# Two mixtures of experts on one core: the first one's last quarter sums in SBUF, and its preparation work is emitted by a model that knows DMA

## The chip, the cores and the metric

The kernel runs on one core of a Trainium2 chip. The metric is the device time of one execution in microseconds (us). Below, TensorE does the matmuls, VectorE and ScalarE work on whole tiles, GpSimd helps with some subtractions and issues some DMAs, and SyncE issues most DMAs.

## The reference

Attention with two kinds of sparse mask (heads 0 to 3 local, heads 4 to 7 strided), then two dense mixtures of experts. All values are float32; the weights come as float64.

```python
x = attention(q, k, v)            # 4 batches x 576 tokens = 2304 tokens, 8 heads x 64 = 512 columns
h = x @ w_in                      # MoE 1: 512 -> 2048
g = h * np.tanh(softplus(h))      # mish
x = g @ w_out                     # 2048 -> 512
g = x @ w_gate                    # MoE 2: 512 -> 1536
val = x @ w_val
out = (silu(g) * val) @ w_out     # 1536 -> 512
```

## The kernel before

**Precision.** Every float32 operand is split into a high part (a rounded copy, made by ScalarE, `split_hi`) and a low part (the difference, made by VectorE or GpSimd, `split_lo`). One product is three matmuls (`mm3`, all recorded at L141): high x high, high x low, low x high.

**Weights.** The weights arrive as 64-bit tiles of 128 x 512. A *raw unit* (`w_ops`) makes one 32-bit tile of one raw tile: four VectorE operations (L348, L351, L356, L359), one squaring on ScalarE (L353), then the split (L131 on ScalarE, L136 on VectorE). A *sum unit* makes a sum or difference tile (`S12`, `S34`) of two weights that are there already: two half-width VectorE operations (L325 to L333), then the split. MoE 2 goes over its weights twice (token halves P = 0 and P = 1), so its units are stored to DRAM when they are first made (`wd`) and fetched again with `ld`.

**Tokens.** They stand in five chunks, four of 512 and one of 256. Chunks 0 and 1 are token half P = 0, chunks 2 and 3 are P = 1. The in-product of a half, a 2 x 2 block product, is done with seven products instead of eight (`PROD`), from sums of inputs (`T1` to `T4`, made by `t_items`) and of weights (`S12`, `S34`). Each of the seven is done for two groups of output columns, so a round holds 14 products in banks X, Y and Z. After the first three, ScalarE copies the bank as it stands (`k`, L986, in MoE 2 L1197); the next product adds to the same bank and must wait for that copy.

**MoE 1** (`middle`) goes over its 2048 inner columns in four quarters of 512. Quarters 1 to 3 hold: a round for one half (`in_round(q, A)`), the small chunk (`small_h`), three output phases (`y_phase`, one for each chunk of that half, then chunk 4), a round for the other half (`in_round(q, Z)`), and two output phases. Quarter 0's sums are stored to DRAM (`yd`); every later output phase copies its four banks with ScalarE (`yv`, L1039) and adds them to `yd` by an accumulating DMA of GpSimd's queue (L1045). The T tiles of a half are stored once and fetched back by ScalarE's queue (`t_load`, L1134) in the output phases ahead of the round that needs them. After the last round the sums are fetched from `yd` (L1114, L1121) and `operand` makes the seven operands of MoE 2's half P = 0 during the last output phase.

**Order of the work.** The instructions are emitted by hand in program order, and each engine and each DMA queue runs them in that order. What is not on TensorE's path stands in a list, `plan`, of raw units, sum units, T sums and gates (a gate holds the list until a stage of TensorE has been emitted). `fill` takes the head of the list as long as its end by a small model (`clk`: TensorE, VectorE and ScalarE, each with fixed costs) is before TensorE's; `need` runs the list on until a given weight is there. The model before has no DMA: a unit may be emitted before its raw tile has landed. `w_load` issues raw tiles from SyncE's queue as slots come free (`raw`, `ws`: two tiles each; a stored unit's target is a `ws` tile too). `W2_QUARTER` says how many units of MoE 2 each quarter takes.

**MoE 2** runs rounds r = 0 to 12; round r computes 256 inner columns of one half (`c_round`, and for P = 0 `c4_round` for chunk 4) and adds the outputs of round r - 1 (`d_tile`, L1261 on VectorE). The 36 units of MoE 2 that MoE 1 has not made are made here, one step behind every product (`w_late_step`; `LATE_ROUND` says how many units each round gets), and what is left is flushed ahead of the next round (`w_late_flush`).

Of the kernel before, what the change touches and what calls it, by code (L numbers as in the profile page):

```python
# [104 lines left out]
def local_strided_attention__mish_moe__swiglu_kernel(  # L105
# [15 lines left out]
    clk = {"pe": 0.0, "dve": 0.0, "act": 0.0}  # L121
# [26 lines left out]
    xh, xl, acc = {}, {}, {}  # L148
    for c, (t0, n) in enumerate(CHUNKS):
        xh[c] = sb.tile([128, 4, n], F32R, tag=f"xh{c}", name=f"xh{c}")  # L150
        xl[c] = sb.tile([128, 4, n], F32R, tag=f"xl{c}", name=f"xl{c}")

    def new_acc(c, a, n):
        acc[c] = sb.tile([128, a, n], F32, tag=f"acc{c}", name=f"acc{c}")
# [10 lines left out]
    w2list = w2_in("g", 0, "W0", "W1", "S12") + w2_out(0) + w2_in("g", 0, "S34") + w2_out(1, 2)  # L165
    w2list += w2_in("v", 0, "W0", "W1", "S12") + w2_out(3) + w2_in("v", 0, "S34") + w2_out(*range(4, 11))
    w2list += w2_in("g", 1, "W0", "W1", "S12") + w2_out(11) + w2_in("g", 1, "S34")
    for i in range(1, NP):
        for kind in "gv"[i == 1:]:
            w2list += w2_in(kind, i, "W0", "W1", "S12", "S34")  # L170
    wlist, plan, rtag = [], [], {}
# [11 lines left out]
    def put_w2(n):  # L183
        for _ in range(n):
            wlist.append(w2list.pop(0))
# [13 lines left out]
    put_w2(W2_QUARTER[0])  # L199
    for q in range(1, NQ):  # L200
# [7 lines left out]
        put_w2(W2_QUARTER[q])  # L208
# [15 lines left out]
    whole = set()  # L224

    def w_load(most=1):
        while most:
# [5 lines left out]
            if i < late["first"]:  # L233
# [8 lines left out]
                raws[i] = sb.tile([128, 512], I64, tag=tag, name="raw", bufs=2)  # L242
            else:
# [33 lines left out]
    def w_dest(i, key):  # L277
        if len(key) == 3:
            if i >= late["first"]:
                return w2_slot(key[0], key[1], key[2])  # L280
            return sb.tile([128, 2, 512], F32R, tag="ws", name="ws", bufs=2)
# [100 lines left out]
    def w_late_step():  # L382
        if not wq:
# [9 lines left out]
        while wq:  # L393
            op = wq.pop(0)
            op()
            if op is not w_hi:
                break

# [286 lines left out]
    def y_out(n, y, e):  # L685
# [9 lines left out]
        {"B11": "xh0", "T1": "xl0", "T2": "xh1", "B22": "xl1", "T3": "xh2", "B21": "xl2", "T4": "xh3"},  # L695
        {"B11": "xl3", "T1": "xh0", "T2": "xl0", "B22": "xh1", "T3": "xl1", "B21": "xh2", "T4": "xl2"},
    )
    tmp = [[], []]

    def operand(P, k):  # L700
# [3 lines left out]
        if k in ("T1", "T3"):  # L704
            tmp[k == "T3"] = [sb.tile([128, 512], F32, tag="pt", name="tt", bufs=4) for _ in range(2)]
        for j in range(2):
            if k[0] == "B":
                src = {"B11": y0[:, j], "B21": y0[:, 2 + j], "B22": y1[:, 2 + j]}[k]
            else:
                src = tmp[k == "T3"][j]  # L710
# [790 lines left out]
```

## Time and profile before

| | |
|---|---|
| median of 3 runs | 895.18 us (892.93 to 897.38) |
| the profiled execution | 891.74 us, of which the span is 890.0 us |
| mean granted clock of TensorE in it | 0.986 |
| busy: TensorE, its weight loads, VectorE, ScalarE, GpSimd | 96%, 80%, 69%, 51%, 21% |
| attention and quarter 0's first part | 0 to 117 us |
| MoE 1, quarters 0 to 3 | 117 to 472 us |
| MoE 2 | 472 to 890 us |

How to read it: the busy share of an engine is a mean over stages with different limits, so it only says who can be the bound. The idle time of TensorE, what ended it, and the granted clock of the same stretch are found in the waits and the windows. The rows are in microseconds from the span's start.

### The profile page before, as it was taken

The page shows a single profiled execution, that of the slowest core. Times are in us where ns is not written, and L with a number is a line of the kernel's source. Part 1 is how long each engine was busy: PE and PEld are TensorE (multiplying, and loading weights), DVE is VectorE, ACT ScalarE, POOL GpSimd, SP SyncE. Part 2 cuts the span into 40 slices and gives each one's busy share as a digit, 9 for nine tenths or more (in the row PEclk, how much of TensorE's full clock was granted, in tenths as well). Part 3 has the DMA queues.
Part 4 walks back from the last instruction along what each step waited for, and adds up shares of the span by engine and source line. Part 5 has one row for each costly group of instructions (what it writes and reads, how often), then busy time and mean ns, then how long its engine had stood idle before and what let it go on. Part 6 is the DMA issues. An engine that isn't in the chain of part 4 may idle for free.

```text
span 890.0 us, 14314 instructions
## 1 busy us (share of the span) xinstructions
PE 858.8 (96%) x5216; PEld 711.9 (80%) x5216; DVE 612.6 (69%) x1334; ACT 455.8 (51%) x1095; POOL 187.2 (21%) x210
## 2 busy tenths in 40 slices
PE   8999999989999989999698999999999999999998
PEld 5787778867888868788487888888888888888886
DVE  6998788667768648595458797978875635333534
ACT  7999955644756447465356544444443422332230
POOL 5643311002010010001014531212224312111211
PEclk9999999989999989999799999999999999999999
DMA  9865335634783694819679637566462563653322
GB/s 289 276 199 172 113 143 213 213 118 78 254 225 83 187 328 137 200 45 298 201 276 296 256 142 264 185 237 196 159 239 92 189 243 117 208 169 139 119 95 95
DMA packets 48166, 166.59 MB, mean 187 GB/s; under 512 B 5216, under 2 KB 8928, under 8 KB 45792
## 3 DMA queue, kind: packets, MB, share of 16 engines
q1 hardware_dynamic: 41328, 134.01, 43.6%
q0 software_dynamic: 5760, 25.17, 11.7%
q10 hardware_dynamic: 1008, 6.50, 2.1%
q8 instruction: 41, 0.67, 0.3%
q14 instruction: 29, 0.24, 0.1%
HBM read 104.32 MB, written 61.34 MB: 186 GB/s over the span
## 4 chain that ended last, share of the span: by engine, by line
PE 79%; DMA 8%; DVE 6%; ACT 4%; issue 1%; SPq 0%; POOL 0%; ACTq 0%; DVEq 0%; POOLq 0%
PE o L141 17%; PE y L141 14%; PE h L141 7%; PE cXg L141 7%; PE cXv L141 7%; PE cX L141 6%; DMA raw<-in_w_dram 5%; PE cZg L141 4%; PE c L141 3%; PE cZv L141 3%; PE cZ L141 3%; PE cYg L141 2%; PE cYv L141 2%; PE cY L141 2%; PE xp L575 1%; PE tp L538 1%
## 5 line engine op out<-in xcount | busy, mean ns | idle before, releaser
L141 PE MATMUL y<-g,w 128*128 128x512 f32 (+1 forms) x960 | 205.9, 372 | 5.6 <-ACT w L131 3.0
L141 PEld LDWEIGHTS y<-g,w 128*128 128x128 f32 x960 | 167.9, 190 | 37.7 <-DVE w L136 4.6
L141 PE MATMUL o<-wr,fs 128*128 128x512 f32 x648 | 149.6, 389 | 0.0
L141 PEld LDWEIGHTS o<-wr,fs 128*128 128x128 f32 x648 | 121.3, 188 | 25.0
L136 POOL TENSOR_TENSOR fs<-k,fs 128x512 fp32r<-128x512 f32 x36 | 49.4, 1372 | 260.2 <-ACT fs L131 181.8
L1261 DVE TENSOR_TENSOR acc<-acc,o 128x512 f32<-128x512 f32 x90 | 61.4, 685 | 36.5 <-PE o L141 36.2
L1045 POOL DMA_DIRECT2D yd<-yv x28 | 23.1, 824 | 293.9 <-ACT yv L1039 293.4
L131 ACT CAST fs<-k 128x512 fp32r<-128x512 f32 x36 | 22.4, 622 | 89.7 <-DVE k L1214 36.7
L141 PE MATMUL h<-xh,w 128*128 128x512 f32 (+1 forms) x208 | 61.5, 360 | 0.0
L141 PE MATMUL cXg<-T,wr 128*128 128x512 f32 x216 | 55.0, 390 | 2.8 <-ACT k L1197 2.8
L492 ACT ACTIVATE pt<-pt,sm 128x64 f32<-128x64 f32 (+1 forms) x160 | 55.9, 361 | 3.3 <-DVE sm L478 3.3
L141 PE MATMUL cXv<-T,wr 128*128 128x512 f32 x216 | 54.8, 389 | 0.0
L1200 DVE TENSOR_TENSOR k<-cZg,k 128x512 f32<-128x512 f32 x12 | 8.3, 692 | 67.0 <-PE cZg L141 67.0
L141 PE MATMUL cX<-xT,w 128*128 128x512 f32 x144 | 38.6, 418 | 12.9 <-ACT k L986 12.9
L141 PEld LDWEIGHTS cXg<-T,wr 128*128 128x128 f32 x216 | 40.4, 188 | 11.7 <-ACT k L1197 3.2
L1039 ACT COPY yv<-y 128x512 f32<-128x512 f32 x56 | 31.1, 589 | 33.4 <-PE y L141 23.1
L141 PEld LDWEIGHTS cXv<-T,wr 128*128 128x128 f32 x216 | 40.6, 188 | 8.4
L141 PEld LDWEIGHTS cX<-xT,w 128*128 128x128 f32 x144 | 28.6, 201 | 20.5 <-ACT k L986 14.5
L141 PEld LDWEIGHTS h<-xh,w 128*128 128x128 f32 x208 | 37.0, 189 | 5.2 <-issue 0.2
L521 POOL TENSOR_TENSOR pt<-pt,sm 128x192 f32<-128x192 f32 (+2 forms) x48 | 34.1, 730 | 16.6 <-DVE sm L514 13.0
L1197 ACT COPY k<-cXg 128x512 f32<-128x512 f32 x24 | 14.1, 589 | 43.8 <-PE cXg L141 43.8
L141 PE MATMUL h<-xl,w 128*128 128x512 f32 (+1 forms) x104 | 36.4, 350 | 0.0
(178 smaller groups left out, 1806.2 us busy)
## 6 DMA issues: line engine op xcount, KB each, us to landing
raw<-in_w_dram SPq DMA_DIRECT2D x50, 512.0 KB, 5.6
yd<-yv POOLq DMA_DIRECT2D x28, 512.0 KB, 8.5
wr<-wd_p SPq DMA_DIRECT2D x24, 512.0 KB, 5.0
rawl<-in_w_dram SPq DMA_DIRECT2D x18, 512.0 KB, 4.6
wr<-wd_g_S SPq DMA_DIRECT2D x16, 512.0 KB, 3.4
wr<-wd_v_S SPq DMA_DIRECT2D x14, 512.0 KB, 4.6
wd_p<-ws SPq DMA_DIRECT2D x12, 512.0 KB, 7.2
wr<-wd_g_W SPq DMA_DIRECT2D x10, 512.0 KB, 6.1
```

The lines of the kernel that those rows point to most:

```text
L131: nc.scalar.copy(hi, src)
L136: eng.tensor_tensor(out=lo, in0=src, in1=hi.bitcast(F32), op=ALU.subtract)
L141: nc.tensor.matmul(o, lhsT=lhs, rhs=rhs, start=first and i == 0, stop=last and i == 2, skip_group_check=more)
L492: nc.scalar.activation(out=pt[:, x], in_=pt[:, x], func=AF.Exp, scale=-1.0, bias=sm[:, 0, x:x + 1], accum_out=sm[:, 1, x:x + 1],)
L521: nc.gpsimd.tensor_tensor(out=a, in0=a, in1=sm[:, 1, x].unsqueeze(2).to_broadcast(a.shape), op=ALU.mult)
L538: nc.tensor.transpose(tp[:, 128 * x:128 * x + 128], a, ident)
L575: nc.tensor.matmul(banks[r][64 * h:64 * h + 64, o:o + nq - skip], lhsT=v_t[s][rows, i, 64 * h:64 * h + 64], rhs=ts[rows, c0 + skip:c0 + nq ...
L1039: on_act(COPY if nt == 512 else 0.4, clk["pe"], lambda: nc.scalar.copy(dst, p[:, :nt]))
L1045: nc.gpsimd.dma_start(yd[c][:, e0:e + 1], src, **kw)
L1197: nc.scalar.copy(t, p)
L1200: nc.vector.tensor_tensor(out=t, in0=p, in1=t, op=ALU.add)
L1261: nc.vector.tensor_tensor(out=acc[c][:, t], in0=acc[c][:, t], in1=o, op=ALU.add)
```

## The change

- **Units.** `W2_QUARTER` (5, 2, 8, 9 units of MoE 2 in MoE 1) gives way to the lists `early`: 2, 2, 6, 4, and 4 more behind the operands in quarter 3. So 18 units are made in MoE 1 instead of 24, and six (out-weights 1, 3, 5, 7, 8, 9) move into MoE 2: `LATE_ROUND` goes from (4, 8, 8, 8, 8) to (4, 9, 9, 9, 9, 2), and two steps follow each of the first three products when P = 0. The first two units are now out-weights 11 and 10, not in-weights and their sums.
- **The model.** `clk` gets SyncE, GpSimd's queue and the DMA engines. `moved` gives the time at which a transfer lands; a unit's first operation is not emitted by `fill` before its raw tile has landed by it, and a stored unit's split not before its target's earlier store has. TensorE's clock now also waits for weights, banks and operands (`pe_at`).
- **T sums.** `t_load` of the next half moves from the output phases into the round ahead (behind its third, fourth and sixth product), still on ScalarE's queue.
- **Quarter 3's sums.** The sums so far are fetched from `yd` ahead of each phase (`y_fetch`), and the phase adds its banks to them in SBUF with VectorE. The copies, the accumulating DMAs, and the fetches after the last round go, as do two 1 MB fetches in rounds 2 and 3 of MoE 2.
- **Operands.** The seven operands of P = 0 become items of `plan` (`op_items`): T1 and B11 behind the gate `y0`, the others behind quarter 3's last round. T2 is made as T3 + B11 instead of from T1. `small_operand` moves from round 0 of MoE 2 to quarter 3. The operands and final sums use other tiles (`SLOT`, `ACC`).
- **Start of MoE 2.** Units left over are filled in during round 0 (`w_rest`); round 1's weights are fetched behind round 0's sixth product.

```diff
-W2_QUARTER = (5, 2, 8, 9)
-LATE_ROUND = (4, 8, 8, 8, 8)
+LATE_ROUND = (4, 9, 9, 9, 9, 2)
+LATE_OUT = ((), (1,), (3,), (5,), (7,), (8, 9))
...
+ISSUE, LAND, MOVE, ADD_MOVE = 0.4, 2.1, 1.55, 2.7
...
+    def moved(queue, ready, halves=1, cost=MOVE):
+        if queue:
+            clk[queue] = max(clk[queue], ready) + ISSUE
+            ready = clk[queue]
+        clk["dma"] = max(clk["dma"], ready) + halves * cost
+        return clk["dma"] + LAND
...
+    early = [
+        w2_out(11, 10),
+        w2_out(0, 2),
+        w2_in("g", 0, "W0", "W1", "S12") + w2_out(4) + w2_in("g", 0, "S34") + w2_out(6),
+        w2_in("v", 0, "W0", "W1", "S12", "S34"),
+        w2_in("g", 1, "W0", "W1", "S12", "S34"),
+    ]
...
+            put_w2(q)
+            plan += [("gate", "y0"), ("op", "T1"), ("op", "B11")]
+            plan += [("gate", ("in", q, 1))] + [("op", k) for k in ("T3", "T2", "T4", "B22", "B21")]
+            put_w2(NQ)
...
     def hi_item(key, w, tf, ready):
+        def at():
+            r, k = slot_of.get(key, ([0, 0.0], 1))
+            return max(ready(), r[k])
+
         def do():
-            t = on_act(0.62, ready(), lambda: split_hi(nc.scalar, w[:, 0], tf))
+            t = on_act(0.62, at(), lambda: split_hi(nc.scalar, w[:, 0], tf))
             held.append((key, w, tf, t))
 
-        return (0.0, lambda: 0.0, do)
+        return (0.0, at, do)
...
-            items.append((cost, lambda: 0.0, do))
+            items.append((cost, lambda k=k: landed.get(i, 0.0) if k == 0 else 0.0, do))
...
+                if q == NQ - 1:
+                    x = acc[c][:, e]
+                    on = lambda: nc.vector.tensor_tensor(out=x, in0=x, in1=p[:, :nt], op=ALU.add)
+                    free(at, on_dve(0.69 if nt == 512 else 0.42, max(clk["pe"], landed["y", c]), on))
+                    continue
...
+    def y_fetch(c, tag, queue, bufs=1):
+        acc[c] = sb.tile([128, 4, CHUNKS[c][1]], F32, tag=tag, name="ys%d" % c, bufs=bufs)
+        (nc.scalar if queue == "act" else nc.sync).dma_start(acc[c], yd[c])
+        landed["y", c] = moved(queue, clk["pe"], 2 if c < NCH - 1 else 1)
...
-            in_round(q, A)
+
+            def behind_a(n):
+                if q > 1 and n in (2, 3, 5):
+                    t_load(Z, {2: "T1", 3: "T2", 5: "T3"}[n])
+
+            def behind_z(n):
+                if last and n == 2:
+                    y_fetch(3, "acc2", "act")
+
+            in_round(q, A, behind_a)
+            if last:
+                y_fetch(0, "xh0", "sp")
+                y_fetch(1, "xh1", "sp")
             small_h(q)
+            if last:
+                y_fetch(4, "v", "sp", 2)
...
+            if last:
+                gates["y0"] = clk["dve"]
             y_phase(q, 4, (0, 1, 2, 3))
-            in_round(q, Z)
+            if last:
+                small_operand()
+            in_round(q, Z, behind_z)
             if last:
                 w_late()
-                for c in (0, 1):
-                    new_acc(c, 4, 512)
-                    nc.sync.dma_start(acc[c], yd[c])
+                y_fetch(2, "acc3", "sp")
...
             if last:
-                drain()
-                new_acc(4, 4, 256)
-                nc.sync.dma_start(acc[4], yd[4])
...
-                at = (("B11", "T1"), ("T2", "B22"), ("T3", "B21"), ("T4",))
-                y_phase(q, 2, (0, 2, 1, 3), lambda i: [operand(0, k) for k in at[i]])
...
+                y_phase(q, 2, (0, 2, 1, 3))
...
                 w_late_step()
+                if n < 3 and P == 0:
+                    w_late_step()
...
-            if r in (2, 3):
-                new_acc(r, 4, 512)
-                nc.sync.dma_start(acc[r], yd[r])
...
                 def between(n):
-                    if r == 0 and n == 3:
-                        small_operand()
+                    if r == 0:
+                        if n == 5:
+                            if rest[0]:
+                                w_rest(True)
+                            ld(1, "W0", "S12", "S34")
+                        return
```

## Rows read from the trace of the kernel before

**Rows 1.** The page, part 1: busy time, share of the span, instructions.

```profile
PE 858.8 (96%) x5216; PEld 711.9 (80%) x5216; DVE 612.6 (69%) x1334; ACT 455.8 (51%) x1095; POOL 187.2 (21%) x210
```

**Rows 2.** Waits of PE, whole run: total us, times, longest us.

```profile
PE cX L141 <- ACT k L986: 12.9, 3, 8.8
PE y L141 <- ACT w L131: 3.0, 1, 3.0
PE cXg L141 <- ACT k L1197: 2.8, 1, 2.8
PE y L141 <- DVE w L136: 2.6, 2, 1.5
PE cZ L141 <- ACT w L131: 1.8, 1, 1.8
```

**Rows 3.** Windows: length; PE, PEld, DVE, ACT, POOL busy; clock, DMA share, GB/s.

```profile
186.72:222.98 36.26, 30.69 (x147) 25.09 (x145) 23.66 (x39) 15.30 (x28) 4.63 (x6) 0.91 0.46 104
223.00:242.05 19.05, 19.05 (x87) 15.76 (x86) 13.98 (x22) 14.28 (x25) 1.43 (x2) 1.00 0.82 291
...
316.88:342.75 25.87, 21.72 (x86) 16.96 (x85) 14.88 (x25) 12.69 (x25) 0.86 (x1) 0.87 0.81 247
...
385.90:419.50 33.60, 33.59 (x194) 29.45 (x192) 22.20 (x37) 15.59 (x29) 2.39 (x3) 1.00 0.64 200
419.50:450.43 30.93, 22.18 (x87) 17.74 (x86) 19.01 (x31) 16.68 (x31) 1.95 (x3) 0.83 0.59 174
450.43:472.19 21.76, 21.76 (x98) 18.02 (x97) 10.78 (x15) 9.75 (x17) 6.80 (x6) 1.00 1.01 340
```

**Rows 4.** The chain that ended last, 386 to 392 us: start, us, what.

```profile
386.06 5.75 PE h L141 x48
```

**Rows 5.** Timeline of ACT: start, us, instruction, idle time before and its releaser.

```profile
322.19 0.62 ACT L131 CAST ws<-wt 128x512 fp32r<-128x512 f32 x1 [5.70 <-DMA wd_v_S<-ws]
...
421.97 0.64 ACT L986 COPY k<-cX 128x512 f32<-128x512 f32 x1
433.52 0.68 ACT L353 ACTIVATE sq<-raw 128x512 f32<-128x512 f32 x1 [10.91 <-DMA raw<-in_w_dram]
```

**Rows 6.** Timeline of SyncE's queue around 184 us.

```profile
183.69 0.32 SPq L760 DMA_DIRECT2D wd_g_S<-ws  x1
184.18 3.64 SPq L248 DMA_DIRECT2D raw<-in_w_dram  x4
```

**Rows 7.** DMA issues, 395 to 436 us: count, KB each, median us to landing.

```profile
raw<-in_w_dram SPq DMA_DIRECT2D x5, 512.0 KB, 10.8
yd<-yv POOLq DMA_DIRECT2D x4, 512.0 KB, 9.6
wd_p<-ws SPq DMA_DIRECT2D x4, 512.0 KB, 9.1
```

**Rows 8.** DMA issues, whole run.

```profile
raw<-in_w_dram SPq DMA_DIRECT2D x50, 512.0 KB, 5.6
...
acc<-yd SPq DMA_DIRECT2D x4, 1024.0 KB, 8.9
...
acc<-yd SPq DMA_DIRECT2D x1, 512.0 KB, 14.8
```

**Rows 9.** VectorE groups (busy us, mean ns): two from 117:480, two from 539.2:693.

```profile
L351 DVE SCALAR_TENSOR_TENSOR wt<-raw,wt 128x512 int32<-128x512 int32 x40 | 27.7, 692 | 1.3
...
L348 DVE TENSOR_SCALAR wt<-raw 128x512 int32<-128x512 int32 x40 | 16.9, 422 | 24.0 <-DMA raw<-in_w_dram 24.0
...
L1261 DVE TENSOR_TENSOR acc<-acc,o 128x512 f32<-128x512 f32 x37 | 25.1, 683 | 3.2 <-PE o L141 2.9
...
L351 DVE SCALAR_TENSOR_TENSOR wt<-rawl,wt 128x512 int32<-128x512 int32 x12 | 11.5, 955 | 0.2
```

**Rows 10.** Windows: one round of MoE 2 (round 3).

```profile
577.60:616.00 38.40, 38.40 (x193) 32.78 (x192) 32.80 (x55) 16.65 (x30) 8.18 (x6) 1.00 0.63 219
```

**Rows 11.** Timeline of VectorE in the same round.

```profile
587.38 0.69 DVE L1200 TENSOR_TENSOR k<-cZg,k 128x512 f32<-128x512 f32 x1 [4.60 <-PE cZg L141]
```

More of the change, by code (lines that the diff above doesn't have):

```diff
@@ L181, in put_sums, with put_w2 @@
             plan.append(("unit",))
-    def put_w2(n):
-        for _ in range(n):
-            wlist.append(w2list.pop(0))
+    def put_w2(x):
+        for key in early[x]:
+            wlist.append(key)
             plan.append(("unit",))
@@ L704, in operand @@
         if k in ("T1", "T3"):
-            tmp[k == "T3"] = [sb.tile([128, 512], F32, tag="pt", name="tt", bufs=4) for _ in range(2)]
+            tmp[k] = [sb.tile([128, 512], F32, tag="pt", name="tt", bufs=4) for _ in range(2)]
         for j in range(2):
@@ L859, in t_items, with op_items, vec_item, pair_items @@
         return with_split(items), lo("T4", z1)
-    t_rest = []
+    def op_items(k):
+        y0, y1 = acc[0], acc[1]
+        t = sb.tile([128, 2, 2, 512], F32R, tag=SLOT[0][k], name=k)
+        ops[0][k] = t
+        if k in ("T1", "T2", "T3"):
+            tmp[k] = [sb.tile([128, 512], F32, tag="pt", name="tt", bufs=4) for _ in range(2)]
+        items = []
+        for j in range(2):
+            if k[0] == "B":
+                src = {"B11": y0[:, j], "B21": y0[:, 2 + j], "B22": y1[:, 2 + j]}[k]
+            else:
+                src = tmp["T2" if k == "T4" else k][j]
+                x3 = tmp["T3"][j] if k != "T1" else None
+                in0, in1, op = {
+                    "T1": (y1[:, j], y0[:, j], ALU.subtract),
+                    "T3": (y1[:, 2 + j], y1[:, j], ALU.subtract),
+                    "T2": (x3, y0[:, j], ALU.add),
+                    "T4": (y0[:, 2 + j], src, ALU.subtract),
+                }[k]
+                items.append(vec_item(src, in0, in1, op))
+            items += pair_items(t[:, j, 0], t[:, j, 1], src, (nc.gpsimd, nc.vector)[j])
+        return items
+    def vec_item(out, in0, in1, op):
+        do = lambda: nc.vector.tensor_tensor(out=out, in0=in0, in1=in1, op=op)
+        return (SPLIT, lambda: 0.0, lambda: on_dve(SPLIT, 0.0, do))
+    def pair_items(hi, lo, src, eng):
+        at = [0.0]
+        def do_hi():
+            at[0] = on_act(0.62, clk["dve"], lambda: split_hi(nc.scalar, hi, src))
+        def do_lo():
+            if eng is nc.vector:
+                on_dve(SPLIT, at[0], lambda: split_lo(eng, lo, src, hi))
+            else:
+                clk["pool"] = max(clk["pool"], at[0]) + 2 * SPLIT
+                split_lo(eng, lo, src, hi)
+        return [(0.0, lambda: 0.0, do_hi), (SPLIT, lambda: at[0], do_lo) if eng is nc.vector else (0.0, lambda: 0.0, do_lo)]
+    def w_rest(last=False):
+        clk["dve"] = max(clk["dve"], clk["pe"] - 0.6)
+        fill()
+        if last:
+            drain()
+        if last or not head() and not behind:
+            assert not head() and not behind and not held
+            rest[0] = None
+            w2_tiles("ws", 2, ("W1", 1, "g"), ("W1", 1, "v"))
+            w2_tiles("raw", 2, ("p", 0), ("p", 1))
+            ld(0, 0, 1)
     def head():
@@ L869, in head @@
             kind, *x = plan[0]
+            if kind == "op" and behind:
+                bg.extend([hi_item(*behind.pop(0)), lo_item()])
+                return bg[0]
             if kind == "gate":
@@ L1061, in middle @@
             clk[k] = 0.0
-        whole.update([("i", QF), ("i", QF + 2)] + [("o", f) for f in range(QF)])
+        for r in turns.values():
+            r[1:] = [0.0, 0.0]
+        landed.update((i, 0.0) for i in list(landed))
+        whole.update((k, 0.0) for k in [("i", QF), ("i", QF + 2)] + [("o", f) for f in range(QF)])
         def h_plain(n, f):
@@ L1153, in ld @@
                 t = w2_slot(kind, r, x)
-                if kind != "p" and P == 0 and i > (kind == "g"):
+                if P == 0 and (2 * i + x in sum(LATE_OUT, ()) if kind == "p" else i > (kind == "g")):
                     continue
```

159 lines of the change are left out of this document (100 added, 59 removed).

## The prediction

> **What bounds the kernel now.** I read the page first. TensorE is busy for 96% of the span [rows 1], so only its idle time, and time at a lower clock, can be won. The waits of TensorE, grouped, say who ended that idle time [rows 2]: ScalarE copies of product banks, 12.9 us in three waits, then splits of weights, 3.0 and 2.6, then a copy at the start of the second mixture of experts (MoE 2), 2.8, then 1.8. Next the stretches of MoE 1. Equal work stands in several of them, so the undisturbed one measures the others [rows 3]. A round of seven products on one token half takes 19.05 us undisturbed; quarter 2's second round takes 25.87 (6.8 lost) and quarter 3's second round 30.93 (11.9 lost). The small chunk's products and three output phases take 33.60 in quarter 3, of which the products are 5.75 [rows 4], so the phases take 27.85; in quarter 1 they take 36.26 (8.4 lost). With the wait of 1.8 ahead of quarter 3 and the 2.8 in round 0 of MoE 2 [rows 2], 8.4 + 6.8 + 1.8 + 11.9 + 2.8 = **31.7 us** are lost. That is more than the waits: in the stretches that hold them the granted clock is 0.91, 0.87 and 0.83 on average and 1.00 in the others [rows 3], so some matmuls ran at the lower of the two levels.
>
> Then what ended those waits. ScalarE stood for 10.91 us before the squaring of a raw weight tile that had not landed [rows 5]; the copy of the next bank was queued behind it, and TensorE waited for that copy. In quarter 2 it stood 5.70 us before a split whose target was still being written to DRAM [rows 5]. In quarter 1 the late raw out-weights were issued at 184.18, right behind a store that SyncE's queue issued at 183.69 [rows 6]. Engines run in order, so an operation emitted before its data is there holds everything behind it. Around quarter 3's wait a raw tile took 10.8 us to land, a store 9.1 and an accumulating store 9.6 [rows 7]; over the whole run a raw tile takes 5.6 [rows 8].
>
> **The change, part by part.** *Fewer units in MoE 1.* A raw unit is 0.42 + 4 x 0.69 = 3.2 us of VectorE [rows 9], a sum unit, two half-width operations and one whole, 2 x 0.42 + 0.69 = 1.5. Ahead of quarter 1 two raw units stand in place of three raw and two sums: 6.4 instead of 12.6 us. The late out-weights may be issued only when every earlier stored unit is split, so their issue at 184.18 moves ahead by these 6.2 or more, and 8.4 shrinks to between 0 and 4 (what a second late tile could cost, 9.6 less the 5.6 of a median one); I take 1.5, nearer to 0, since 6.2 is most of 8.4. In quarter 2 six units stand for eight, in quarter 3 four (and four behind the operands) for nine: in each a megabyte or more read, and as much stored, leaves the stretch in which raw tiles took 10.8.
>
> *Emission by a model with DMA.* A unit enters the engines' order only when the model says that its raw tile has landed (0.4 + 1.55 + 2.1 = 4.05 us, plus its queue) or that its target's store is done. Where that comes true no copy is held; where DMA is later than the model, it is held for the difference. It has slack: a round of 19.05 us is 14 products of 1.36, and a bank's copy is made after the first of them and needed before the fifth, so 3 x 1.36 less the copy's 0.64 [rows 5] = 3.4 us. At the median of 5.6 the error is 1.6 and hidden; at 10.8 it is 6.7, and 3.3 of it show. Quarter 2's 6.8 becomes 0 to 6.8; I take 2.5, nearer to the median. The wait of 1.8 comes behind output buffers whose accumulating stores are not finished; quarter 2 keeps these stores, so it stays.
>
> *Sums in SBUF in quarter 3.* Nine accumulating stores and 20 ScalarE copies go; 16 VectorE additions of 0.683 [rows 9] and 4 half-width ones of about 0.42 come, 12.6 us over 33.60 + 19.05 + 21.76, in which VectorE is busy for 22.20, 13.98 (the undisturbed round) and 10.78 [rows 3]. That is room enough, and units leave besides. Their cover is that the five old sums are there in time. Such a fetch took 8.9, and 14.8 at worst [rows 8]; the first two are issued at the end of a round, 5.75 + 27.85/2.5 = 16.9 us before the first phase's end, where its additions stand. If the cover is gone, a late sum holds VectorE and with it four banks. SyncE waits for the round's end before these fetches, and raw tiles queue behind them, whose users are a phase later. Quarter 3's 11.9 becomes 0 to 6 (half, if the second of two late tiles stays); I take 2.
>
> *T sums fetched during products.* The three 1 MB fetches move on ScalarE's own queue from the output phases into the round ahead, each issued when its tile's last reader is a product old, so that nothing behind it is held; they leave the phases where raw tiles and accumulating stores compete. The Trainium skill, "DMA: Bandwidth & Descriptors", section "Issuing engines are not separate DMA queues", says that transfers started by any engine run on the same 16 DMA engines and interleave. By that rule their queue hides nothing, only the earlier time does, and quarter 2 could keep its whole 6.8, the upper end above; the trace's 10.8 beside other queues' transfers agrees with it.
>
> *Operands of MoE 2.* The first two are made inside quarter 3's last round, the others during its last two phases, from sums that are whole since quarter 3's first half; before, all seven stood in the last phase and ended in the 2.8 wait. Count and kind of the operations stay. 2.8 becomes 0 to 2.8; I take 1, because units that are left now overlap round 0, and round 1's fetched weights are issued only after its sixth product, 2.72 + 5.75 = 8.5 us ahead of use, where a raw tile of that size takes 5.6.
>
> *Six units later.* Rounds 1 to 4 of MoE 2 get one more raw unit each. A round is 38.40 us with VectorE busy for 32.80 in 55 instructions [rows 10]. Five more are 3.0 us at that mean, and 4.8 if each took the 0.955 that L351 takes there [rows 9]: 35.8 to 37.6, under 38.40. An idle 4.60 us of VectorE [rows 11] lies in the first three products, where the change puts two steps for one. So 0, or at worst 1 per round; I take 1 in all, and 1 more for left steps flushed ahead of round 1. The Trainium skill, "SBUF — State Buffer", section "Who interferes with whom", says that a VectorE operation with two SBUF inputs contends with a GpSimd one that reads SBUF. By that rule L351's 0.955, against 0.692 in MoE 1, is such waiting, and a unit put where GpSimd is idle costs 3.2; the sum would stay.
>
> **Sum.** Left are 1.5 + 2.5 + 1.8 + 2 + 1 + 1 + 1 = 10.8 us, so 20.9 go. The profiled execution took 891.74 (890.0 of it span), which gives 870.8. The median of the runs is 895.18, 3.4 above it; as a third of the waits stays, I keep a third of that: **872.0**. Bounds: with all 31.7 gone 860.0; with the upper ends left (4 + 6.8 + 1.8 + 6 + 2.8 + 4 + 1 = 26.4) 886.4, and with the same share of 3.4, 889. What is late next is then TensorE itself.
>
> **The rivals.** *The model is too early.* Its 4.05 against 10.8 leaves 3.3 us per raw tile on TensorE, and as a wait of 8.8 [rows 2] lost 11.9 in all, 4.4 with the clock. Three such tiles in quarters 2 and 3 add 13: 885. For it: the accumulating stores of quarters 1 and 2 stay. Against: fewer bytes there. *It doesn't do what it says.* The order of emission comes out much as before, since a matmul that needs a unit forces it anyway, and a wait for the forced weight takes the place of each wait for a copy: about 893. Against: the raw tile that cost 10.91 was for a unit that only MoE 2 reads. *Slower.* The plan is a strict list, and a head that the model holds back holds the weights behind it. In quarter 2 six units share two target tiles: three turns of a store and a raw tile, at 9.1 + 10.8, are 60 us of the 33.60 + 19.05 + 21.76 = 74 in which four raw and four sum units for quarter 3 must follow (18.8 us). From 74 on they come as a burst ahead of a round, with TensorE waiting for all of it; in two quarters that is 37.6 on 872, about 909. Against: eight units fitted into the same stretch before.
>
> **How the numbers follow.** Chances: the forecast (861 to 881) 0.65, the model too early (881 to 889) 0.19, no effect 0.08, slower 0.08. About 0.5%, 4.5 us, is what a measurement of this kernel can tell from no change; so faster 0.84, same 0.08, slower 0.08. The range 861 to 889 leaves out the last two and a little below.
>
> **What would show it.** In the new profile: quarter 3's second round at 19 to 21 us, and no ScalarE wait of over 5 us for a raw tile; the out-weights of quarter 1 issued well before 184; additions of 0.69 on VectorE in quarter 3 and no accumulating store; rounds 1 to 4 at 38.4 with VectorE busy for 36 to 37. Wrong would be waits of VectorE for the fetched sums, rounds above 39, or the same waits for other tiles.

## The result, and the profile after

The changed kernel takes **865.46 us** (median of 4 runs, 863.77 to 871.11). The kernel before, measured beside it, takes 894.28 (892.93 to 897.38). The ratio is 0.9684 (95% interval 0.963 to 0.9738), a gain of 28.8 us. The profiled execution of after is the longest of its four: 871.11 us, of which the span is 869.3, at a mean granted clock of 0.994; the other three took 863.77 to 866.90, at 0.998 to 1.000. Against the 891.74 of before's profiled execution it gained 20.6. All rows of after below are of this longest execution.

The page of after, part 1 (busy time, share of the span, instructions), answers to [rows 1]:

```profile
PE 855.0 (98%) x5216; PEld 710.7 (82%) x5216; DVE 619.6 (71%) x1354; ACT 448.5 (52%) x1075; POOL 177.2 (20%) x201
```

ScalarE has 20 instructions fewer and VectorE 20 more: the copies and additions of quarter 3. Next the waits of TensorE in after, from 117 to 700 us (total us, times, longest us), beside [rows 2]:

```profile
PE cXg L160 <- DVE k L1344: 4.7, 2, 3.3
PE cXg L160 <- DMA wr<-wd_g_W: 1.0, 1, 1.0
...
PE cZ L160 <- ACT w L150: 0.6, 1, 0.6
```

The waits of 12.9, 3.0, 2.8 and 2.6 are gone. Of the kind that was 1.8 ahead of quarter 3 (`cZ`, a weight's split), 0.6 stands in quarter 2. Waits stand there that before did not have, in MoE 2 (`cXg`), for VectorE and for a fetched weight. The windows of after (length; busy PE, PEld, DVE, ACT, POOL; clock, DMA share, GB/s) answer to [rows 3] and [rows 10]: quarter 1's phases, quarter 2's second round, quarter 3's phases and second round, then rounds 1 and 2 of MoE 2.

```profile
190.40:217.95 27.55, 27.55 (x146) 23.79 (x145) 21.86 (x37) 13.99 (x26) 5.14 (x7) 1.00 0.50 105
312.40:331.40 19.00, 19.00 (x85) 15.73 (x85) 9.23 (x14) 13.15 (x23) 0.86 (x1) 1.00 0.58 177
378.40:406.00 27.60, 27.60 (x147) 23.76 (x146) 22.15 (x39) 9.87 (x18) 1.30 (x1) 1.00 0.46 169
406.10:425.20 19.10, 19.10 (x86) 15.80 (x85) 9.93 (x17) 13.44 (x24) 4.97 (x5) 1.00 0.16 56
471.80:517.10 45.30, 40.92 (x193) 34.03 (x194) 40.36 (x69) 19.45 (x37) 9.23 (x7) 0.96 0.66 239
517.10:555.50 38.40, 38.40 (x194) 32.77 (x193) 36.00 (x61) 17.79 (x33) 7.76 (x6) 1.00 0.58 206
```

The 36.26 of quarter 1 is 27.55, the 25.87 of quarter 2 is 19.00, the 30.93 of quarter 3 is 19.10, and the clock is back at 1.00 in all three. Round 1 of MoE 2 stands out: 45.30 for the 38.40 that the next round takes.

The table sets every kernel of this study against the undisturbed length of each stage (in its heading, us), from the starts of TensorE's groups. What stands in it is time lost; blank is under 0.3. "q2 2nd" is quarter 2's second round, and so on; "r0" is round 0's in-products with its chunk 4, "r1" round 1's in-products, "r2, r3" those of rounds 2 and 3 together. Two losses lie outside its columns: 0.8 in quarter 2's first round in after, and the in-products of round 5, 1.7 in after and 1.7 to 2.1 in the other kernels with the units moved, but 4.5 in the last row. The stages are those of the one profiled execution of each kernel, the median is of all its executions.

| kernel | q1 phases 27.54 | q2 2nd 19.07 | q3 1st 19.47 | q3 2nd 19.07 | last phases 21.76 | r0 24.79 | r1 19.04 | r2, r3 38.08 | median us |
|---|---|---|---|---|---|---|---|---|---|
| before | 8.7 | 6.8 | 1.9 | 11.9 | | 3.8 | | | 894.28 |
| **after** | | | | | | 1.1 | 5.8 | | 865.46 |
| e1 no model | | | | | | 0.6 | 3.6 | | 866.71 |
| e2 model alone | 7.5 | | 8.4 | | 4.4 | 13.8 | | | 893.86 |
| e3 T fetches late | | | | | | 1.0 | 4.9 | | 866.33 |
| e4 units back | 7.1 | | 4.5 | | | 6.9 | 1.6 | | 880.49 |
| e5 sums in DRAM | | | | | | 4.9 | | 3.6 | 868.40 |
| e6 out-weight 1 early | | | | | | 2.1 | | | 863.86 |
| e7 units alone | | 2.2 | | 9.1 | | 5.9 | | 3.2 | 881.15 |
| e8 five units first | 7.6 | | | | | 0.9 | 5.7 | | 874.53 |
| e9 units, model | | 0.4 | | | 4.9 | 13.7 | | 2.8 | 882.81 |
| e10 units, sums | | 2.3 | 0.3 | | | 1.1 | 5.8 | | 868.89 |
| e11 fetch order | | | | | | | 1.8 | | 863.12 |
| e12 units, T fetches | | | | 4.1 | | 4.9 | | 3.9 | 875.35 |

### The profile page after: what moved, and what is told of

Same layout as the page of the kernel before. It is cut to its first block, busy times and chain, and to the rows that moved or that the text cites. A ratio compares the mean times of both kernels' runs of the same rounds, so it can differ in the third digit from the quotient of the medians.

```text
span 869.3 us, 14259 instructions
## 1 busy us (share of the span) xinstructions
PE 855.0 (98%) x5216; PEld 710.7 (82%) x5216; DVE 619.6 (71%) x1354; ACT 448.5 (52%) x1075; POOL 177.2 (20%) x201
## 4 chain that ended last, share of the span: by engine, by line
PE 87%; issue 5%; DMA 3%; DVE 2%; ACT 1%; POOL 1%; SPq 0%; POOLq 0%; ACTq 0%; DVEq 0%
PE y L160 18%; PE o L160 17%; PE h L160 8%; PE cXg L160 7%; PE cXv L160 7%; PE cX L160 6%; PE c L160 4%; PE cZv L160 4%; PE cZg L160 3%; PE cZ L160 3%; PE cYv L160 2%; PE cYg L160 2%; PE xp L617 2%; PE tp L580 2%; PE cY L160 2%
## 5 line engine op out<-in xcount | busy, mean ns | idle before, releaser
L160 PE MATMUL y<-g,w 128*128 128x512 f32 (+1 forms) x960 | 202.3, 369 | 0.0
L1173 POOL DMA_DIRECT2D yd<-yv x20 | 16.1, 803 | 189.2 <-ACT yv L1167 189.2
L1167 ACT COPY yv<-y 128x512 f32<-128x512 f32 x40 | 23.0, 589 | 29.1 <-PE y L160 23.3
L563 POOL TENSOR_TENSOR pt<-pt,sm 128x192 f32<-128x192 f32 (+2 forms) x48 | 33.8, 724 | 17.9 <-DVE sm L556 11.9
L155 DVE TENSOR_TENSOR wr<-wt,wr 128x512 fp32r<-128x512 f32 x42 | 33.7, 801 | 5.1 <-ACT wr L150 5.0
L150 ACT CAST wr<-wt 128x512 fp32r<-128x512 f32 x42 | 25.8, 614 | 22.1 <-DVE wt L370 12.9
```

Source lines behind the costliest of these rows:

```text
L150: nc.scalar.copy(hi, src)
L155: eng.tensor_tensor(out=lo, in0=src, in1=hi.bitcast(F32), op=ALU.subtract)
L160: nc.tensor.matmul(o, lhsT=lhs, rhs=rhs, start=first and i == 0, stop=last and i == 2, skip_group_check=more)
L563: nc.gpsimd.tensor_tensor(out=a, in0=a, in1=sm[:, 1, x].unsqueeze(2).to_broadcast(a.shape), op=ALU.mult)
L1167: t = on_act(COPY if nt == 512 else 0.4, clk["pe"], lambda: nc.scalar.copy(dst, p[:, :nt]))
L1173: nc.gpsimd.dma_start(yd[c][:, e0:e + 1], src, **kw)
```

## The experiments

Two theories were put to the test first. **M:** the emission by a model that knows DMA wins the time, by keeping a unit out of the engines' order until its data is there. **U:** the amount of work wins it, since six fewer units in MoE 1, and two instead of five ahead of quarter 1, leave room whatever the order. Sums in SBUF and T fetches are smaller parts by both.

**The model taken out** of the changed kernel: nothing lands late by the model, and no unit waits for it.

```diff
     def moved(queue, ready, halves=1, cost=MOVE):
-        if queue:
-            clk[queue] = max(clk[queue], ready) + ISSUE
...
+        return 0.0
...
-        return (0.0, at, do)
+        return (0.0, lambda: 0.0, do)
```

> The changed kernel with the model's DMA taken out: transfers cost nothing in it, a unit is emitted whether its raw tile has landed or not, TensorE's clock waits for nothing. Units, sums in SBUF and early fetches stay. Theory M (the order of emission is what won MoE 1's time): the ScalarE waits for raw tiles come back, quarter 2's and 3's second rounds are 4 to 12 us over 19.05 again and the median is 875 to 890. Theory U (fewer units and fewer bytes won it): rounds stay at 19 to 21, the median within 4 us of 865.5.

866.71 us (865.0 to 867.55), ratio 0.97 (0.9679 to 0.972): within about a microsecond of the changed kernel. With all other parts there, the model is not needed.

**The model alone**, put into the kernel before (24 units in the order before, DRAM sums, T fetches in the phases, one step behind each product).

```diff
-            items.append((cost, lambda: 0.0, do))
+            items.append((cost, lambda k=k: landed.get(i, 0.0) if k == 0 else 0.0, do))
```

> The kernel before with the model alone: 24 units in MoE 1, accumulating stores in all quarters, fetches of T sums in the output phases, operands in the last phase, one step behind every product in MoE 2. Theory M: 15 to 25 us of the 28.8 are won with it, the median is 870 to 880, and what stays lost is the 1.8 ahead of quarter 3 and the 2.8 at the start of MoE 2. Theory U: 0 to 8 us are won, 886 to 894.

893.86 us (891.39 to 896.58), ratio 1.0006 (0.9993 to 1.002). Waits of TensorE, 121 to 600 us:

```profile
PE cXg L160 <- ACT k L1335: 7.9, 1, 7.9
PE cXg L160 <- ACT B L150: 4.3, 1, 4.3
PE y L160 <- ACT w L150: 2.9, 1, 2.9
PE cX L160 <- ACT w L150: 2.8, 1, 2.8
```

The second rounds of quarters 2 and 3 run undisturbed, as intended, and ScalarE's waits for raw tiles in MoE 1 fall from 27.7 us in before to 1.3. But 7.5 us stay in quarter 1, 8.4 appear ahead of quarter 3, 4.4 in the last phases and 13.8 at the start of MoE 2: TensorE waits there for splits of weights (the last two lines), an operand and a copy. The held units come later, and the same time is lost there. Theory M falls.

**24 units in MoE 1 again**, with all other parts of the change.

```diff
-LATE_ROUND = (4, 9, 9, 9, 9, 2)
-LATE_OUT = ((), (1,), (3,), (5,), (7,), (8, 9))
+LATE_ROUND = (4, 8, 8, 8, 8)
+LATE_OUT = ((),) * 6
...
-        w2_out(11, 10),
-        w2_out(0, 2),
+        w2_in("g", 0, "W0", "W1", "S12") + w2_out(0) + w2_in("g", 0, "S34"),
+        w2_out(1, 2),
```

> The changed kernel with the units as before: 5, 2, 8, 9 of MoE 2 in the four quarters (five of the last behind the operands), 4 and four times 8 in MoE 2's rounds 0 to 4. Theory M: MoE 1 loses 0 to 5 us, and round 1 of MoE 2, which took 45.3 in the changed kernel, is back near 38.4 to 40, so the median is 860 to 868. Theory U: MoE 1 loses 10 us or more in quarters 1 to 3, the median is 872 to 885.

880.49 us (879.52 to 881.19), ratio 0.9855 (0.984 to 0.987): 15 us are lost again, in quarter 1 (7.1), ahead of quarter 3 (4.5) and in round 0 (6.9). So the units decide more than any other part that was taken out. The edit changes two things, how many units there are and which come first; the kernel with five units first, below, takes the second alone.

**Quarter 3's sums in DRAM again**: accumulating stores, the fetches after the last round and in rounds 2 and 3, the operands in the last phase, and the start of MoE 2 as before. In this run and in the later one that adds the sums in SBUF, these go together; no run takes them apart.

```diff
-                if q == NQ - 1:
-                    x = acc[c][:, e]
-                    on = lambda: nc.vector.tensor_tensor(out=x, in0=x, in1=p[:, :nt], op=ALU.add)
-                    free(at, on_dve(0.69 if nt == 512 else 0.42, max(clk["pe"], landed["y", c]), on))
-                    continue
...
+                y_phase(q, 2, (0, 2, 1, 3), lambda i: [operand(0, k) for k in at[i]])
```

> The changed kernel with quarter 3's sums added in DRAM again, fetched behind its last round, and the operands made in its last output phase; model, units and early T fetches stay. Theory M: quarter 3's second round stays at 19 to 22 us, only the 2.8 at the start of MoE 2 and a little more come back: 866 to 872. Theory S (the accumulating stores of quarter 3 are what made its raw tiles late): that round is 5 to 12 us longer, 873 to 882.

868.4 us (867.19 to 870.93), ratio 0.9724 (0.9704 to 0.9745). Quarter 3 stays undisturbed, so theory S of the text above does not hold with the other parts there; round 0 loses 4.9, and rounds 2 and 3, which fetch two of the sums, 3.6, while round 1 gains its 5.8 back, though it has the ninth unit too.

**Five units ahead of quarter 1**, 18 in all as in the changed kernel.

```diff
-        w2_out(11, 10),
-        w2_out(0, 2),
+        w2_in("g", 0, "W0", "W1", "S12") + w2_out(0) + w2_in("g", 0, "S34"),
+        w2_out(2, 4),
```

> The changed kernel with one thing altered: which of its 18 units of MoE 1 come ahead of quarter 1. Five (three raw, two sums, the selection of the kernel before) instead of two; as many fewer later (5, 2, 3, 4 and 4). All else stays: model, T fetches, sums in SBUF. Theory U (the work put ahead of a stage decides): quarter 1's phases, 27.53 us in the changed kernel, are again 34.6 to 36.3, as in the kernel before (36.26) and with the units put back (34.64), so 7 to 8 us are lost: 872 to 874. Theory M (the emission model keeps work away from a stage that has no room): phases below 30, time 864 to 868.

874.53 us (873.2 to 875.85), ratio 0.9781 (0.9763 to 0.98). Its quarter 1 in a window, and SyncE's queue in it and then in after:

```profile
187.60:222.70 35.10, 30.17 (x146) 25.00 (x146) 25.98 (x43) 15.81 (x29) 5.16 (x7) 0.90 0.48 107
```

```profile
184.52 0.32 SPq L807 DMA_DIRECT2D wd_g_S<-ws  x1
185.00 3.65 SPq L284 DMA_DIRECT2D raw<-in_w_dram  x4
```

```profile
171.12 0.33 SPq L807 DMA_DIRECT2D wd_p<-ws  x1
171.61 3.94 SPq L284 DMA_DIRECT2D raw<-in_w_dram  x4
```

Five units put the four raw out-weights behind a store at 184.52, as in [rows 6]; with two they go at 171.61. That one list is worth 9 us of the 15 that the units put back had cost, and the model, which is on in this kernel, does not help it.

**The units alone**, put into the kernel before with the second step behind the first products.

```diff
-W2_QUARTER = (5, 2, 8, 9)
-LATE_ROUND = (4, 8, 8, 8, 8)
+LATE_ROUND = (4, 9, 9, 9, 9, 2)
+LATE_OUT = ((), (1,), (3,), (5,), (7,), (8, 9))
...
+                if n < 3 and P == 0:
+                    w_late_step()
```

> The kernel before with the units alone: the changed lists (2, 2, 6, 4 and 4 in MoE 1; six later, two steps behind the first products), no model of DMA, T fetches in the output phases, quarter 3's sums in DRAM, operands in the last phase. Theory U: the units carry nearly all of the gain; quarter 1's phases 27.5, rounds of quarters 2 and 3 below 21, time 868 to 873. If T fetches, model and sums are needed as well (each hidden when taken alone because the others cover for it), quarter 3's second round stays above 24 and the time is 876 to 885.

881.15 us (880.34 to 883.0), ratio 0.9858 (0.9839 to 0.9878): 13 of the 29 us, not nearly all. Quarter 1 is cured, quarter 3's second round is not. SyncE's queue, ScalarE and TensorE around it:

```profile
401.24 3.46 SPq L800 DMA_DIRECT2D wd_v_S<-ws  x2
```

```profile
414.93 0.62 ACT L146 CAST ws<-wt 128x512 fp32r<-128x512 f32 x1 [7.19 <-DMA wd_v_S<-ws]
```

```profile
416.09 4.89 PE L156 MATMUL cX<-xT,w 128*128 128x512 f32 x12 [6.86 <-ACT k L1096]
```

This is the mechanism of [rows 5], with a store for the raw tile: a split that waits 7.19 us for its target's store (the second of the two in the first line), a bank's copy behind it, and TensorE 6.86 us for the copy. No wait of ScalarE for a raw tile is left in its MoE 1 (27.7 us in before); 34.6 us of waits for stores of units are (14.2 in before). Theory U as stated is too simple; with the units moved, quarter 3 still needs a second remedy. Which of the other parts is one, the next three kernels tell: the units with the model, with the sums in SBUF, and with the early T fetches.

**Units and model.**

```diff
+        return (0.0, at, do)
...
-            items.append((cost, lambda: 0.0, do))
+            items.append((cost, lambda k=k: landed.get(i, 0.0) if k == 0 else 0.0, do))
```

> The kernel before with two parts of the change: the units moved and the emission model of DMA. T fetches in the output phases, quarter 3's sums in DRAM, operands in the last phase, as before. The units alone gave 881.15 us, with 28.12 us in quarter 3's second round, where ScalarE stood 7.19 us before a split whose target was still being stored. If the model is a second, sufficient remedy for that (it knows of stores): this round 19 to 21, time 867 to 873. If the model only moves the wait, as it did with all 24 units: round at 19 to 21, but the last phase and round 0 of MoE 2 longer by as much, time 877 to 884.

882.81 us (881.5 to 883.12), ratio 0.9872 (0.9852 to 0.9892). Quarter 3's second round is undisturbed and the time is the same: 4.9 us stand in the last phases and 13.7 in round 0. ScalarE and SyncE's queue of this kernel, and its DMA issues from 420 to 447 us (count, KB each, median us to landing):

```profile
446.21 0.62 ACT L150 CAST ws<-wt 128x512 fp32r<-128x512 f32 x1 [13.83 <-DMA wd_g_W<-ws]
```

```profile
428.25 0.32 SPq L805 DMA_DIRECT2D wd_g_W<-ws  x1
430.75 0.32 SPq L805 DMA_DIRECT2D wd_g_S<-ws  x1
```

```profile
acc<-yd SPq DMA_DIRECT2D x2, 1024.0 KB, 7.5
...
wr<-wd_v_S SPq DMA_DIRECT2D x2, 512.0 KB, 14.7
...
wd_g_W<-ws SPq DMA_DIRECT2D x1, 512.0 KB, 17.9
```

Of the held units' stores two were issued only behind the fetches of sums and weights after the last round. The store at 428.25 landed 17.9 us later, and ScalarE stood 13.83 us for it. In the code `ld` and these sum fetches pass no time to the model, so by it the store takes 0.4 + 1.55 + 2.1 = 4.05 us.

**Units and sums in SBUF**, no model, T fetches late.

```diff
+            plan += [("gate", "y0"), ("op", "T1"), ("op", "B11")]
+            plan += [("gate", ("in", q, 1))] + [("op", k) for k in ("T3", "T2", "T4", "B22", "B21")]
...
+                if q == NQ - 1:
+                    x = acc[c][:, e]
```

> The kernel before with two other parts: the units moved, and quarter 3's sums in SBUF with the operands in the plan. No model, T fetches in the output phases. If taking nine accumulating stores and 20 copies out of quarter 3 is a sufficient remedy for the 28.12 us round of the units alone: round at 19 to 21, round 0 at 19 to 20, time 866 to 870. If the early T fetches were needed for it: round above 23, time 873 to 880.

868.89 us (866.65 to 870.74), ratio 0.9718 (0.9694 to 0.9742): 12.3 us under the units alone. This is a second remedy that is enough by itself. By the stages it takes 9.1 out of quarter 3's second round, 4.8 out of round 0 and 3.2 out of rounds 2 and 3, and brings 5.8 into round 1.

**Units and early T fetches**, no model, sums in DRAM.

```diff
+            def behind_a(n):
+                if q > 1 and n in (2, 3, 5):
+                    t_load(Z, {2: "T1", 3: "T2", 5: "T3"}[n])
```

> The kernel before with two parts: the units moved and the T sums fetched in the round ahead. No model; quarter 3's sums in DRAM, operands in the last phase. Known: the units alone 881.15 us, units and model 882.81, units and sums 868.89, units with model and T fetches 868.4. If the early T fetches are by themselves the other remedy: quarter 3's second round at 19 to 21, round 0 of MoE 2 at 22 to 24, time 867 to 871, and the model is worth nothing here. If they need the model: second round above 24, time 877 to 884, and model and T fetches are worth about 13 us together where the sums stay in DRAM.

875.35 us (874.31 to 876.31), ratio 0.9791 (0.9767 to 0.9816), between the two expectations: half a remedy, 5.8 us, with 4.1 left in quarter 3's second round. The other 7 come when the model is added (868.4, the run with DRAM sums above, which differs from this one by the model alone), though the model added to the units by itself won nothing. By the stages the 7 are these 4.1 and 2.5 in round 5. In quarter 3 the wait is again for a store; in all of MoE 1 ScalarE waits 24.4 us for stores of units here, and not at all with the model:

```profile
408.63 0.62 ACT L146 CAST ws<-wt 128x512 fp32r<-128x512 f32 x1 [6.29 <-DMA wd_v_S<-ws]
```

The cause of the 2.5 in round 5 stays open.

**T fetches late**, in the otherwise changed kernel.

```diff
             def behind_a(n):
-                if q > 1 and n in (2, 3, 5):
-                    t_load(Z, {2: "T1", 3: "T2", 5: "T3"}[n])
+                return
```

> The changed kernel with the T sums fetched in the output phases again, as before. Theory U: their 3 MB fit either way once units have left, time 865 to 868, no wait of TensorE in quarter 2 above 2 us. If the earlier fetch matters: waits for late raw tiles return in quarter 2 (its second round above 21), 869 to 874.

866.33 us (864.77 to 867.85), ratio 0.969 (0.9668 to 0.9711): no measurable difference. Where the sums are in SBUF, the fetches fit either way.

**Round 1's ninth unit taken out**, a raw one: out-weight 1 is made in quarter 3. (The eight and nine of the text below count all units of the round, raw and sum.)

```diff
-LATE_ROUND = (4, 9, 9, 9, 9, 2)
-LATE_OUT = ((), (1,), (3,), (5,), (7,), (8, 9))
+LATE_ROUND = (4, 8, 9, 9, 9, 2)
+LATE_OUT = ((), (), (3,), (5,), (7,), (8, 9))
...
-        w2_in("v", 0, "W0", "W1", "S12", "S34"),
+        w2_in("v", 0, "W0", "W1", "S12", "S34") + w2_out(1),
```

> The changed kernel with one unit moved back: out-weight 1 is made in quarter 3 (five units there), and round 1 of MoE 2 has 8 raw units again instead of 9. In the changed kernel round 1 takes 45.3 us instead of 38.4, with waits for raw tiles that were issued behind round 1's stored weights. If the ninth raw tile is what round 1 lacks room for: round 1 at 38.4 to 40, quarter 3 unchanged, time 859 to 862. If it is the start of the stretch (raw tiles queued behind the fetched weights) and not the number: round 1 stays above 43 and the time is 864 to 867. If quarter 3 has no room for a fifth unit: its last round goes from 19.07 to above 21, and the time is 864 or above.

863.86 us (862.66 to 865.42), ratio 0.9667 (0.9649 to 0.9684). Round 1's products take 19.18 instead of 24.83, and quarter 3 is undisturbed. Round 0 loses 1 us more than in after, in a wait of 1.94 for a fetched weight, so of 6.9 us 2.2 are left. The median lies above the 859 to 862 that were expected for this outcome.

**The fetches' order changed as well**: the out-weights that are read a round later are fetched last.

```diff
-            ld(0, 0, 1)
...
                             ld(1, "W0", "S12", "S34")
+                            ld(0, 0, 1)
```

> The changed kernel with out-weight 1 made in quarter 3, and at round 0's end the stored in-weights of round 1 fetched ahead of the out-weights of round 0, which are read a round later. With out-weight 1 in quarter 3 alone the time was 863.86 us, with 1.94 us of TensorE waiting for a fetched in-weight at round 1's start. If SyncE's order sets that wait: below 0.8 us, c4 and round 1 together 25.0 to 26.0 instead of 27.03, time 861 to 863.5. If the transfers' load sets it: the wait stays, time 863 to 865.

863.12 us (862.12 to 865.92), ratio 0.9663 (0.9638 to 0.9689). Windows of round 0's in-products with chunk 4, and of round 1:

```profile
443.40:468.20 24.80, 24.80 (x133) 21.50 (x132) 18.78 (x30) 14.73 (x26) 7.13 (x5) 1.00 0.36 133
468.20:508.60 40.40, 39.59 (x195) 32.67 (x194) 38.35 (x65) 18.36 (x35) 9.31 (x7) 1.00 0.74 283
```

The wait for the fetched weight is gone, so SyncE's order did set it, but 1.8 us of it appear in round 1, where VectorE makes the last weights: chunk 4's products and round 1 are together 26.58, not the 25 to 26 expected. By their stages the two kernels are about 5 us shorter there than after's profiled execution; by the medians they are 1.6 and 2.3 shorter than after, with overlapping intervals. The two executions of after at a granted clock of 1.000 took 863.77 and 864.03, inside the 862.66 to 865.42 of the first of them. That they beat it is not shown, and how much of round 1's 5.8 the shorter executions of after lose is not known.

## Why the prediction was right, and where its steps were not

The predicted 872.0 lies 6.5 us above the measured 865.46, and the direction and the range held. The steps behind it held less well, and that their sum came out is luck.

**The sum.** 10.8 us were to stay of the 31.7. (By the table it is 33.1 that before had lost: round 0 has 3.8 where its one wait of 2.8 was counted.) The profiled execution of after has lost 0.8 in quarter 2's first round (20.22 for 19.46), 1.1 and 5.8 around round 1, and 1.7 in round 5 (20.79 for 19.09; two units were put there, and the three kernels without them have 19.07 to 19.09): 9.4 us. The totals agree and the places do not. MoE 1's remainder (1.5 + 2.5 + 1.8 + 2) was forecast too high: 0.8 is left of 7.8. MoE 2 was forecast too low: 8.6 instead of 3. Of these 3, the 1 for its start came out as worked out, 1.1 in a wait for one of round 1's fetched weights (`wd_g_W`, 1.0 above). The two units of round 5 were given no price. The forecast of 870.8 for the profiled execution is met by 871.11 for a second accidental reason: 3.7 us of it are a longer start (last section).

**Quarter 1** went as worked out. Fewer units moved the raw out-weights from 184.18 [rows 6] to 171.61, and the whole 8.7 went; the kernel with five units first shows that it was this list, with 18 units and the model in place.

**The emission by a model** got most of the credit for quarter 2, and part of that for quarter 3. That step failed as a cause. The model alone is worth 0 (893.86), taking it out costs about 1 us (866.71), no more than the runs scatter, and with the units it wins nothing (882.81). It wins clearly in one place only, 7 us with the units and early T fetches while the sums are in DRAM (875.35 to 868.40). "Where that comes true no copy is held" was right for the stretch looked at, but a held unit has to be made somewhere, and the step did not ask where. The prediction's own sign, no ScalarE wait of over 5 us for a raw tile, came true in the units alone, which has no model. The rival "it doesn't do what it says", 893, describes the model alone to a microsecond. The rival "slower", a strict list whose held head piles up the rest, describes its mechanism: 13.7 us at the start of MoE 2 rather than the 37.6 priced there.

**What did cure quarters 2 and 3** was fewer units, which ended the waits for raw tiles, and then one of two further steps against the waits for stores. These are medians with the units moved (881.15 by themselves):

| units moved, and | T fetches late | T fetches early |
|---|---|---|
| sums in DRAM, no model | 881.15 | 875.35 |
| sums in DRAM, model | 882.81 | 868.40 |
| sums in SBUF, no model | 868.89 | 866.71 |
| sums in SBUF, model | 866.33 | 865.46 |

Without the model, sums in SBUF win 12.3 us beside late T fetches and 8.6 beside early ones; with it 16.5 and 2.9. Early T fetches win 5.8 (no model) or 14.4 (model) while the sums are in DRAM, and 0.9 to 2.2 beside sums in SBUF, no more than the runs scatter. So three of the parts share one gain of some 15 us, and no sum of parts taken alone gives it. The working gave each stretch one cause and added; 13 + 12 + 6 would have been 31. That the shared thing is the load of transfers is argued from the waits for stores, and not shown: the sums in SBUF also take 20 copies from ScalarE and move the operands.

**The sums' cover** held: no wait of VectorE for a fetched sum appears in after. The additions are the group below (durations in ns, least, median and most):

```profile
L1156 DVE TENSOR_TENSOR ys<-ys,y x20: 420/687/689, 387.5 to 447.0; 128x512 f32<-128x512 f32 x16, 128x256 f32<-128x256 f32 x4
```

16 at 0.687 and four at 0.42 were worked out as 0.683 and 0.42. No ScalarE wait for a raw tile is left in after's MoE 1. Its longest one for a unit's store is this one, which TensorE did not feel, so the rival "the model is too early" found little in the changed kernel:

```profile
396.64 0.62 ACT L150 CAST ws<-wt 128x512 fp32r<-128x512 f32 x1 [3.11 <-DMA wd_v_W<-ws]
```

**The 1.8 ahead of quarter 3** was to stay, since quarter 2 keeps its accumulating stores. It went in every kernel with the units moved, the units alone included, and grew to 4.5 with the units put back. Those stores alone are not its cause.

**T fetches.** The Trainium skill, "DMA: Bandwidth & Descriptors", section "Issuing engines are not separate DMA queues", says that transfers started by any engine run on the same 16 DMA engines and interleave. That agrees with the runs as far as they go: the queue was ScalarE's before and after, and 5.8 us came with the earlier time alone. No run moved the fetches to another queue. Quarter 2's second round keeps 2.2 of its 6.8 with the units alone, and nothing with early T fetches added.

**Units in MoE 2** split in two. Rounds 2 to 4 are as predicted: 38.40 with VectorE at 36.00, so with a ninth unit a round has 36.00 - 32.80 = 3.2 us more of VectorE, inside the 3.0 to 4.8 given. That is a difference of rounds and not the price of a unit where GpSimd is idle, which the prediction also put at 3.2: other operations changed with it. The operation of L351 in [rows 9], 0.955 there, takes 0.690 in round 2 of after (L388), and the low parts of the weights go the other way, 0.684 in before's round 3 (first line) and 0.807 in after's round 2:

```profile
L136 DVE TENSOR_TENSOR wr<-wt,wr 128x512 fp32r<-128x512 f32 x8 | 5.4, 684 | 0.0
```

```profile
L155 DVE TENSOR_TENSOR wr<-wt,wr 128x512 fp32r<-128x512 f32 x10 | 8.1, 807 | 1.3 <-ACT wr L150 1.3
```

The Trainium skill, "SBUF — State Buffer", section "Who interferes with whom", says that a VectorE operation with two SBUF inputs contends with a GpSimd one that reads SBUF. Both of these have two, and GpSimd is busy for 8.18 and 7.76 us of the two rounds, so the rows are in line with it; no run takes GpSimd's work away.

Round 1 is the term that was mis-sized, 2 us forecast for the rounds and the flush, 5.8 measured in it, and "rounds above 39", one of the prediction's signs of being wrong, came true there (45.30). VectorE, ScalarE, TensorE and SyncE's queue of after in round 1:

```profile
488.20 0.43 DVE L385 TENSOR_SCALAR wt<-rawl 128x512 int32<-128x512 int32 x1 [3.18 <-DMA rawl<-in_w_dram]
```

```profile
488.26 0.68 ACT L390 ACTIVATE wr<-rawl 128x512 fp32r<-128x512 f32 x1 [4.17 <-DMA rawl<-in_w_dram]
```

```profile
493.11 1.13 PE L160 MATMUL cXg<-T,wr 128*128 128x512 f32 x3 [3.26 <-DVE k L1344]
```

```profile
466.94 0.71 SPq L1303 DMA_DIRECT2D wr<-wd_g_W  x1
467.75 1.68 SPq L1303 DMA_DIRECT2D wr<-wd_g_S  x2
469.53 0.60 SPq L284 DMA_DIRECT2D rawl<-in_w_dram  x1
...
480.34 0.33 SPq L284 DMA_DIRECT2D rawl<-in_w_dram  x1
```

The raw tile issued at 480.34 was there at 488.2, 7.9 us later, with VectorE and ScalarE waiting 3.18 and 4.17 in order, and behind them a bank's addition for which TensorE waited. Round 1 has 69 VectorE instructions where round 2 has 61: with the units left from round 0 it makes more than nine, and its first raw tile is issued only behind round 1's weights. One unit less ended it (19.18). Nine by themselves fit: the four kernels with the units moved and the sums in DRAM also put nine into round 1, and its in-products take 19.07 in each. So it is the ninth unit together with the start of MoE 2 that comes with the sums in SBUF, the leftovers and the later loads; which of these two is not taken apart. The prediction counted VectorE's time for this and priced neither the raw tile's queue nor the leftovers beyond 1 us.

## What to carry to other kernels

A planner that holds work back until its data is there wins only if the held work finds a free place later; ask for that place first, and look for the loss at the next point where everything must be done. Parts that relieve the same waits (here those of the in-order ScalarE for stores) overlap: their gains taken one at a time neither add up nor show which is needed, so test them with the largest part kept fixed. When work moves into a stage with spare engine time, count also what must be loaded for it and what is queued ahead of that load.

## What was not expected of the hardware

The start, attention and quarter 0's first part, in which the kernels do the same work, ended between 116.7 and 121.2 us in the profiled executions. The eight kernels with quarter 3's sums in SBUF, whose tiles are laid out otherwise, have 117.8 to 121.2, the six others 116.7 to 117.5. The longest is after's own profiled execution, with a granted clock of 0.92 from 20 to 60 us where before's has 1.00:

```profile
20.00:60.00 40.00, 40.00 (x647) 30.74 (x647) 35.66 (x205) 37.68 (x192) 22.08 (x32) 0.92 0.77 250
```

These 3.7 us more than before's 117.5 are part of why after's profiled execution gained 20.6 us and its median 28.8. The four executions of after differ in time from 863.77 to 871.11 and in granted clock from 1.000 to 0.994, the longest at the lowest, so one kernel's executions differ by up to 7 us; how much of that lies in the start is not recorded. Whether the layout adds the microseconds by which the eight starts are longer stays open, since each kernel was profiled once.

In the kernel with units and model, a store of 512 KB issued behind 6 MB of fetches took 17.9 us to land, while the DMA engines moved 329 GB/s (428.25 to 446.20); stores from the same kind of tile took 9.1 in [rows 7].
